# Stage A weights in runs of four columns, and loads moved ahead of the z writes, in a fused FFT-mixing and squared-ReLU kernel

## Chip, cores, metric

The kernel runs on one core of one Trainium2 chip. The metric is device time in microseconds (us), lower is better.

## The reference

x is (8, 3008, 256). It is filtered along the sequence in the frequency domain, then goes through a feed-forward layer:

```python
X = np.fft.rfft(x, axis=1)
Y = X * (filt_r + 1j * filt_i)[None, :, :]
y = np.fft.irfft(Y, n=3008, axis=1).astype(np.float32)      # (8, 3008, 256)
h = np.maximum(y.reshape(24064, 256) @ w_in, 0.0)           # 2048 wide
out = h * h @ w_out                                         # (24064, 256)
```

## The kernel before

The FFT of length 3008 = 64 x 47 is done by matmuls. Stage A transforms over 47, stage B over 64; the product with the filter follows, then stage P (back over 64) and stage y (back over 47). Between A and B and between P and y the data change their layout; for batches 1 to 7 both times through DRAM (u written to dU and read as ut; z written to dZ and read as zt), for batch 0 the first time on chip (uT, turned by TensorE). Batch 0 and part of batch 1 form a prologue. After it, slots of one eighth of a 512-token group follow each other: four matmuls of the first layer (`ffn_g1`), eight of the second for the group before (`ffn_g2`), a ReLU on ScalarE, a square on VectorE. The FFT of batch b+1 is woven into the slots of batch b by `fft_plan`: `put(r, place, unit, ...)` puts a unit into slot r.

Stage A of batch 0, whose casts out of PSUM the change touches:

```python
def chunk_a0(c):
    for k in range(2):
        for dt in range(2):
            if dt == 0:
                banks, _ = bank_pair(f"psA_0_{c}_{k}")       # psH: one tile of two banks; psF, psO: two tiles
            ps = banks[dt]
            for i in range(4):                               # 8 matmuls of 96 columns
                ...
                nc.tensor.matmul(o, xw16[(0, 2 * (c % 2))][:, m, d], s0[:, c // 2, :], start=True, stop=False)
                nc.tensor.matmul(o, xw16[(0, 1)][0:120, m, d], s0[0:120, 2 + c, :], start=False, stop=True)
            m = 32 * c + 16 * k
            o = uT[:, dt, :, m:m + 16].rearrange("p c (m q) -> p m q c", q=4)
            pv = ps[:, 0:384].rearrange("p (m q c) -> p m q c", m=4, q=4)
            if dt == 0: nc.scalar.copy(out=o, in_=pv)
            else:       nc.vector.tensor_copy(out=o, in_=pv)
```

The end of the prologue, and a frequency unit of batch 1 (twelve of them):

```python
for r in range(14):                          # filter, product and stage P of batch 0
    ...                                      # unit_p(0, p) writes z after every third p (4 writes)
    for k in {5: (0,), 8: (1, 2)}.get(r, ()):
        load_wide(1, k); cast_wide(1, k, nc.gpsimd)          # x of batch 1
    if r == 10:
        read_z(0, 0, (0,)); load_wout(0)
... # chunk_a(1, 0..3) between z reads, u writes, load_wout(1) and the first four unit_y(0, n)

def unit_b(b, p):
    ps = psF(...)                                            # two buffers, shared with stages P, y, A
    ... # two matmuls
    nc.vector.tensor_mul(out=prod, in0=ps..., in1=sF[...])
    if b > 0:
        swap = nc.gpsimd if b == 1 else nc.vector
        swap.tensor_copy(out=yf[0:64], in_=prod[64:128, 1])
        swap.tensor_copy(out=yf[64:128], in_=prod[0:64, 1])
def unit_s(b, p):                                            # in the same slot
    nc.vector.tensor_add(out=yf, in0=prod[:, 0], in1=yf)
```

Of the kernel before, what the change touches and what calls it, by code (L numbers as in the profile page):

```python
# [9 lines left out]
F16 = mybir.dt.float16  # L10
# [8 lines left out]
N1, N2, NC, NM = 64, 47, 24, 32  # L19
# [7 lines left out]
def _build_consts():  # L27
    N = N1 * N2
    n2 = np.arange(N2)
    m = np.arange(NM)  # L30


    SA = np.zeros((N2, 2, 2, 2, NC))
    for c in range(NC):
        for h in range(2):
            SA[:, h, h, 0, c] = np.cos(2 * np.pi * n2 * c / N2)
            SA[:, h, h, 1, c] = np.sin(2 * np.pi * n2 * c / N2)



    S0 = np.zeros((128, 6, 2, 48))
    for h in range(2):
        q = SA[:, h, h].reshape(N2, 48)
        for t in range(2):
            S0[2 * h + t::4, t, h] = q[:32]
        for c in range(4):
            S0[4 * h + c:120:8, 2 + c, h] = q[32:]


    freq = np.full((NC, 64), -1)  # L50
    for c in range(NC):
        for j in range(32):
            freq[c, j] = 47 * j + c
            if c:
                freq[c, 32 + j] = 47 * j + 47 - c
    freq[0, 32] = N // 2


    SB = np.zeros((NM, 2, 2, NC, 2, 64))

    n1j = 8 * (m % 8) + 2 * (m // 8)
    SP = np.zeros((2, 64, NC, 2, 2, NM))
    for c in range(NC):
        for f in range(64):
            k = freq[c, f]
            if k < 0:
                continue
            sg = 1.0 if (f < 32 or c == 0) else -1.0
            for h in range(2):
                th = 2 * np.pi * ((k * (32 * h + m)) % N) / N  # L70
                SB[:, h, 0, c, 0, f] = np.cos(th)
                SB[:, h, 1, c, 0, f] = -sg * np.sin(th)
                SB[:, h, 0, c, 1, f] = -np.sin(th)
                SB[:, h, 1, c, 1, f] = -sg * np.cos(th)
            if c == 0 and f == 32:
                SB[:, :, 1, c, :, f] = 0.0
            w = (1.0 if k in (0, N // 2) else 2.0) / N
            for i in range(2):
                th = 2 * np.pi * ((k * (n1j + i)) % N) / N
                cs, sn = w * np.cos(th), w * np.sin(th)  # L80
                SP[0, f, c, i, 0] = cs
                SP[0, f, c, i, 1] = sg * sn
                SP[1, f, c, i, 0] = -sn
                SP[1, f, c, i, 1] = sg * cs


    SY = np.zeros((32, 2, 2, N2, 2))
    for c in range(NC):
        th = 2 * np.pi * c * n2 / N2
        for i in range(2):  # L90
            SY[c + c // 12 * 4, i, 0, :, i] = np.cos(th)
            SY[c + c // 12 * 4, i, 1, :, i] = -np.sin(th)


    PF = np.zeros((128, 6, 2, 2, 32))
    for w, (s, q) in enumerate(PQ):
        for j in range(32):
            PF[4 * j + q, w, :, s, j] = 1.0

    SPx = SP.reshape(2, 64, -1)[::-1]  # L100
    f16 = lambda a, p: np.ascontiguousarray(a.reshape(p, -1).astype(np.float16))
    C0 = np.zeros((128, 896))
    C0[:, 0:576] = S0.reshape(128, 576)
    C0[0:94, 576:672] = SA.reshape(94, 96)
    C0[:, 672:766] = SY.reshape(128, 94)
    C0[:, 768:896] = np.eye(128)
    return f16(C0, 128), f16(PF, 128), f16(SB, 128), f16(SP, 128), f16(SPx, 128)


@with_exitstack  # L110
def kernel(
# [9 lines left out]
    nc = tc.nc  # L121
# [77 lines left out]



    sC0 = const.tile([128, 896], F16, name="sC0")
    nc.scalar.dma_start(out=sC0, in_=dC0.ap())
    s0 = sC0[:, 0:576].rearrange("p (w q) -> p w q", q=96)
    sSA = sC0[0:94, 576:672]
    sSY = sC0[0:112, 672:766]
    ident = sC0[:, 768:896]
# [44 lines left out]
    nc.vector.memset(sign[64:128], -1.0)  # L252


    zero = const.tile([128, 512], F16, name="zero")
    nc.vector.memset(zero, 0.0)

    def keep_warm(n):
        ps = psO("warm").rearrange("p a d -> p (a d)")
        for _ in range(n):  # L260
            nc.tensor.matmul(ps, zero[:, 0:128], zero, start=True, stop=True)

    nc.scalar.copy(out=zero[0:1, 0:1], in_=zero[0:1, 1:2])
    keep_warm(14)


    sF = const.tile([128, 2, NC, D], F16, name="sF")
# [48 lines left out]
        nc.sync.dma_start(out=w32s[2][:, c, :],  # L316
                          in_=moe_w_out.rearrange("(jt r) c -> r jt c", r=128)[:, c, :])

    def cast_wout(k, eng=nc.vector):
        c = slice(4 * k, 4 * k + 4)  # L320
        eng.tensor_copy(out=sWout[:, c, :], in_=w32s[2][:, c, :])


    x16s, us, uts, prods, zes, zts, yts = {}, {}, {}, {}, {}, {}, {}
# [11 lines left out]
    def unit_a(b, a):  # L336

        c, i = divmod(a, 4)
        if i == 0:
            us[(b, c)] = p_u.tile([96, 8, D], F16, tag="u", name=f"u_{b}_{c}")  # L340
        ps = psF(f"psA_{b}_{a}")
        nc.tensor.matmul(ps[0:96, :], sSA, x16s[(b, c)][:, 2 * i:2 * i + 2, :],  # L342
                         start=True, stop=True)
        o = us[(b, c)][:, 2 * i:2 * i + 2, :]
        pv = ps[0:96, :].rearrange("p (a d) -> p a d", d=D)
        if a % 2 == 0:
            nc.scalar.copy(out=o, in_=pv)  # L347
        else:
            nc.vector.tensor_copy(out=o, in_=pv)  # L349
        if i == 3:  # L350
            write_u(b, c)

    def chunk_a(b, c):

        u = p_u.tile([96, 8, D], F16, tag="u", name=f"u_{b}_{c}")
        us[(b, c)] = u
        for k in range(2):
            banks, groups = bank_pair(f"psA_{b}_{c}_{k}")
            for i in range(2):
                m = slice(4 * k + 2 * i, 4 * k + 2 * i + 2)  # L360
                o = banks[i][0:96]
                nc.tensor.matmul(o, s0[:, c // 2, :], xw16[(b, 2 * (c % 2))][:, m, :],
                                 start=True, stop=False)
                nc.tensor.matmul(o, s0[0:120, 2 + c, :], xw16[(b, 1)][0:120, m, :],
                                 start=False, stop=True)
            eng = pair_engine()
            for t, i in groups:
                n = t.shape[1]
                o = u[:, 4 * k + 2 * i:4 * k + 2 * i + 2 * n, :]
                pv = t[0:96].rearrange("p t (a d) -> p (t a) d", d=D)  # L370
                if eng is nc.scalar:
                    eng.copy(out=o, in_=pv)
                else:
                    eng.tensor_copy(out=o, in_=pv)
# [5 lines that stand above are left out]
# [9 lines left out]
                    nc.tensor.matmul(o, xw16[(0, 1)][0:120, m, d], s0[0:120, 2 + c, :],  # L389
                                     start=False, stop=True)  # L390
                m = 32 * c + 16 * k
                o = uT[:, dt, :, m:m + 16].rearrange("p c (m q) -> p m q c", q=4)
                pv = ps[:, 0:384].rearrange("p (m q c) -> p m q c", m=4, q=4)
                if dt == 0:
                    nc.scalar.copy(out=o, in_=pv)  # L395
                else:
# [89 lines left out]
    def unit_y(b, n):  # L486
# [11 lines left out]
                yps[0] = psH(f"psY_{b}_{n}")  # L498
            ps = yps[0][:, dt, :]
        if prologue[0]:  # L500
            nc.tensor.matmul(ps[:, 0:D], zero[:, 0:128], zero[:, 0:D], start=True, stop=True)
        for jj in range(4):
            nc.tensor.matmul(ps[:, 94 * jj:94 * jj + 94],  # L503
                             zt[:, 4 * (g % 2) + jj, dt * 128:(dt + 1) * 128],
# [70 lines left out]
    def fft_plan(b):  # L575
# [6 lines left out]
        if b == 1:  # L582
            for n in range(4, 16):
                put(n - 1 if n < 8 else 10 + n // 2 if n < 12 else 4 * n - 31, n % 2,
                    unit_y, 0, n)
            for k in range(2, 4):
                put(2 + k, 1, cast_wout, k)
        t0 = 6
        for a in range(0 if b > 1 else 16, 16):
            put(t0 + a // 2, a % 2, unit_a, b, a)  # L590
        put(4 if b == 1 else 14, 1, read_u, b)
        t0 = 8 if b == 1 else 18
        for p in range(12):
            r = t0 + (25 if b == 1 else 19) * p // 11
            put(r, 0, unit_b, b, p)
            put(r, 0, unit_s, b, p)
            put(r + 2, 1, unit_p, b, p)
# [48 lines left out]
    uts[0] = p_ut.tile([128, NC, D], F16, tag="ut", name="ut_0")  # L646
    for k in range(6):
        turn_u(k)
    for k, eng in enumerate((nc.vector, nc.scalar, nc.vector)):
        place_f(0, k, eng)  # L650
    place_f(1, 0, nc.scalar)
    for r in range(14):
        if r < 12:
            unit_b(0, r)
        if r < 10 and r % 2 == 0:
            place_f(1, r // 2 + 1, nc.scalar)
        if r < 6 and r % 2 == 1:
            place_f(0, r // 2 + 3, nc.scalar)
        if r >= 2:
            unit_p(0, r - 2)  # L660
        for k in {5: (0,), 8: (1, 2)}.get(r, ()):
            load_wide(1, k)
            cast_wide(1, k, nc.gpsimd)
        if r == 10:
            read_z(0, 0, (0,))
            load_wout(0)
    for k in range(2):
        cast_wout(k, nc.gpsimd)
    read_z(0, 1, (0,))
    chunk_a(1, 0)  # L670
    chunk_a(1, 2)
    for c in range(2):
        read_z(0, c, (1,))
    write_u(1, 0)
    chunk_a(1, 1)
    write_u(1, 2)
    load_wout(1)
    for n in range(2):
        unit_y(0, n)
    chunk_a(1, 3)  # L680
    for n in range(2, 4):
        unit_y(0, n)
    prologue[0] = False
    write_u(1, 1)
    write_u(1, 3)
    for c in range(2, 4):
        read_z(0, c)

# [48 lines left out]
```

## Time and profile before

| | kernel before |
|---|---|
| median of 3 runs, us | 832.46 (829.75 to 833.49) |
| span of the profiled run | 829.0 |
| first ReLU of the feed-forward part | 82.80 |
| slot 8 begins / slot 34 begins / slot 56 begins | 91.87 / 147.97 / 194.70 |

A slot is taken to begin with its ReLU on ScalarE. The page's first lines follow (span; then for each engine busy us, share of the span, instructions). PE is TensorE and PEld its weight loads, DVE is VectorE, ACT ScalarE, POOL GpSimd:

```profile
span 829.0 us, 14766 instructions
PE 790.5 (95%) x6086; PEld 559.4 (67%) x6086; DVE 553.9 (67%) x869; ACT 564.8 (68%) x708; POOL 37.1 (4%) x51
```

TensorE is busy for 95 % of the span.

### The profile page before, as it was taken

How to read it: one execution, taken by the hardware profiler on the slowest of the kernel's cores; microseconds unless marked ns; L12 is line 12 of the kernel's file. 1: busy time of each engine (PE TensorE's matmuls, PEld its weight loads, DVE VectorE, ACT ScalarE, POOL GpSimd, SP SyncE). 2: the span in 40 equal slices, each digit the busy share in tenths (PEclk: the TensorE clock that was granted, in tenths of full speed). 3: DMA queues.
4: the chain of work that ended last, by engine and by line, in shares of the span. 5: the costliest groups of instructions: out<-in, count | busy, mean ns of one | idle time of the engine just before them, and what ended most of it. 6: DMA issues, size and time to landing. Idle time of an engine off the chain costs nothing.

```text
span 829.0 us, 14766 instructions
## 1 busy us (share of the span) xinstructions
PE 790.5 (95%) x6086; PEld 559.4 (67%) x6086; DVE 553.9 (67%) x869; ACT 564.8 (68%) x708; POOL 37.1 (4%) x51
## 2 busy tenths in 40 slices
PE   5686989999999999999999999999999999999998
PEld 3563566666767667786767766786767766676666
DVE  5672766656995589756995579755996569654332
ACT  4572766676777777776777767777777767766663
POOL 4202122000000000000000000000000000000000
PEclk7597999999999999999999999999999999999999
DMA  9449416724563356625555336815556242331111
GB/s 365 172 147 272 153 51 173 173 64 153 141 183 84 102 153 160 172 57 160 153 140 115 95 122 166 201 42 152 145 146 153 64 153 77 101 79 39 39 40 51
DMA packets 87947, 107.95 MB, mean 130 GB/s; under 512 B 6224, under 2 KB 78672, under 8 KB 83408
## 3 DMA queue, kind: packets, MB, share of 16 engines
q1 hardware_dynamic: 87528, 106.59, 45.2%
q8 instruction: 47, 0.77, 0.4%
q10 hardware_dynamic: 288, 0.43, 0.2%
q14 instruction: 20, 0.16, 0.1%
q0 software_dynamic: 64, 0.00, 0.0%
HBM read 58.76 MB, written 48.23 MB: 129 GB/s over the span
## 4 chain that ended last, share of the span: by engine, by line
PE 83%; DMA 6%; DVE 6%; ACT 2%; POOL 1%; issue 1%; SPq 0%; DVEq 0%; POOLq 0%; ACTq 0%
PE psO L548 36%; PE psH L533 35%; PE psA L342 3%; PE psY L503 2%; PE psB L426 2%; DMA ut<-dU 2%; PE psP L462 2%; DVE prod L429 2%; DVE h L541 2%; DMA dZ<-ze 2%; ACT uT L395 1%; DMA xw<-in_x_dram 1%; DMA zt<-dZ 1%; POOL yf L438 1%; POOL yf L437 1%; DVE uT L397 1%
## 5 line engine op out<-in xcount | busy, mean ns | idle before, releaser
L537 ACT ACTIVATE h<-psH 128x1024 f16<-128x1024 f32 x376 | 385.1, 1025 | 191.3 <-PE psH L533 191.3
L548 PE MATMUL psO<-sWout,h 128*128 128x256 f16 x3008 | 388.9, 272 | 0.1
L533 PE MATMUL psH<-yt,sWin 128*128 128x512 f16 (+7 forms) x1728 | 387.1, 351 | 1.9 <-DVE yt L512 1.0
L548 PEld LDWEIGHTS <-h 128*128 128x128 f16 x3008 | 290.6, 98 | 77.9 <-DVE h L541 0.4
L541 DVE TENSOR_TENSOR h<-h 128x1024 f16<-128x1024 f16 x376 | 253.5, 685 | 99.8 <-ACT h L537 98.5
L533 PEld LDWEIGHTS <-sWin 128*128 128x128 f16 x1728 | 159.6, 98 | 101.7 <-issue 3.7
L429 DVE TENSOR_TENSOR prod<-psB,sF 128x1024 f16<-128x1024 f32 x96 | 116.7, 1220 | 10.7 <-PE psB L426 7.6
L512 DVE CAST yt<-psY 128x376 f16<-128x376 f32 x64 | 35.1, 549 | 59.9 <-PE psY L503 55.2
L464 ACT CAST ze<-psP 128x512 f16<-128x512 f32 x96 | 56.0, 586 | 23.3 <-PE psP L462 20.0
L349 DVE CAST u<-psA 96x512 f16<-96x512 f32 x48 | 33.0, 687 | 45.1 <-PE psA L342 45.1
L555 ACT COPY ost<-psO 128x512 f32<-128x512 f32 x94 | 55.4, 589 | 7.7 <-PE psO L548 6.2
L444 DVE TENSOR_TENSOR yf<-prod,yf 128x512 f16<-128x512 f16 x84 | 35.7, 425 | 19.4 <-POOL yf L438 17.0
L503 PE MATMUL psY<-sC,zt 112*128 112x94 f16 x512 | 42.6, 206 | 5.5 <-DMA zt<-dZ 5.3
L503 PEld LDWEIGHTS <-zt 112*128 112x128 f16 x512 | 35.2, 98 | 18.2 <-DMA zt<-dZ 4.8
L426 PE MATMUL psB<-ut,sSB 128*128 128x256 f16 x192 | 36.6, 272 | 2.7 <-DMA ut<-dU 1.3
L342 PE MATMUL psA<-x,sC 94*96 94x512 f16 x96 | 36.6, 382 | 0.0
L426 PEld LDWEIGHTS <-sSB 128*128 128x128 f16 x192 | 18.6, 98 | 23.9 <-issue 4.9
L462 PE MATMUL psP<-yf,sSP 128*128 128x256 f16 x168 | 32.1, 273 | 2.7 <-DVE prod L429 1.8
L510 ACT CAST yt<-psY 128x376 f16<-128x376 f32 x64 | 29.8, 467 | 6.0 <-issue 5.1
L328 DVE CAST x<-x 94x2048 f16<-94x2048 f32 x24 | 29.2, 1217 | 0.0
L347 ACT CAST u<-psA 96x512 f16<-96x512 f32 x48 | 27.5, 572 | 0.0
L395 ACT CAST uT<-psA 128x384 f16<-128x384 f32 x8 | 14.5, 1996 | 13.8 <-PE psA L389 13.8
(56 smaller groups left out, 289.9 us busy)
## 6 DMA issues: line engine op xcount, KB each, us to landing
x<-in_x_dram SPq DMA_DIRECT2D x20, 768.0 KB
dZ<-ze SPq DMA_DIRECT2D x32, 384.0 KB
zt<-dZ SPq DMA_DIRECT2D x64, 192.0 KB
dU<-u SPq DMA_DIRECT2D x28, 384.0 KB
out_dram<-ost SPq DMA_DIRECT2D x32, 256.0 KB
out_dram<-ost SPq DMA_DIRECT2D x64, 128.0 KB
ut<-dU SPq DMA_DIRECT2D x7, 1024.0 KB
xw<-in_x_dram SPq DMA_DIRECT2D x6, 1024.0 KB
```

Source lines behind the costliest of these rows:

```text
L342: nc.tensor.matmul(ps[0:96, :], sSA, x16s[(b, c)][:, 2 * i:2 * i + 2, :], start=True, stop=True)
L426: nc.tensor.matmul(ps[:, i * D:(i + 1) * D], sSB[:, 2 * p + i, :], uts[b][:, 2 * p + i, :], start=True, stop=True)
L429: nc.vector.tensor_mul(out=prod, in0=ps.rearrange("p (a d) -> p a d", d=D).unsqueeze(1).to_broadcast([128, 2, 2, D]), in1=sF[:, :, 2 * p:2 ...
L444: nc.vector.tensor_add(out=yf, in0=prod[:, 0], in1=yf)
L462: nc.tensor.matmul(ps[:, i * D:(i + 1) * D], sSP[:, c2, :], prod[:, i, :], start=True, stop=True)
L464: nc.scalar.copy(out=zes[(b, c)][:, 2 * i6:2 * i6 + 2, :], in_=ps.rearrange("p (a d) -> p a d", d=D))
L503: nc.tensor.matmul(ps[:, 94 * jj:94 * jj + 94], zt[:, 4 * (g % 2) + jj, dt * 128:(dt + 1) * 128], sSY, start=True, stop=True)
L533: nc.tensor.matmul(ps[:, i, o:o + n], sWin[:, dt, jt * 128:(jt + 1) * 128], yts[b][:, dt, r:r + n], start=(dt == 0), stop=(dt == 1))
L537: nc.scalar.activation(out=h2[:, 2 * s:2 * s + 2, :], in_=ps, func=AF.Relu)
L541: nc.vector.tensor_mul(out=v, in0=v, in1=v)
L548: nc.tensor.matmul(pso[g][:, t % 2, :], h2s[g][:, jt, t * 128:(t + 1) * 128], sWout[:, jt, :], start=(jt == 0), stop=(jt == NJT - 1))
L555: nc.scalar.copy(out=ost, in_=pso[g])
```

## The change

The change has three intents: let the casts of batch 0's stage A write runs of four elements, and keep the clock up to it; fetch and cast all of batch 1's x and of W_out before the z writes, so that no load stands between those; and move the fourth chunk of batch 1's stage A out of the prologue into the slots, which makes its u, and so the twelve frequency units, later.

```diff
-    C0[:, 0:576] = S0.reshape(128, 576)
+    C0[:, 0:576] = S0.reshape(128, 6, 2, 2, NC).transpose(0, 1, 4, 2, 3).reshape(128, 576)
+    C0[:, 896:1472] = S0.reshape(128, 576)          # s1, the old order, for batch 1
...
-    keep_warm(14)            # matmuls of 512 columns
+    keep_warm(125)           # of 128 columns
...
-                o = uT[:, dt, :, m:m + 16].rearrange("p c (m q) -> p m q c", q=4)
-                pv = ps[:, 0:384].rearrange("p (m q c) -> p m q c", m=4, q=4)
+                o = uT[:, dt, :, m:m + 16].rearrange("p c (m q) -> p m c q", q=4)
+                pv = ps[:, 0:384].rearrange("p (m c q) -> p m c q", m=4, q=4)
...                                                   # fft_plan, b == 1
-            for k in range(2, 4):
-                put(2 + k, 1, cast_wout, k)           # was on VectorE
+        t0 = 2 if b == 1 else 6
+        for a in range(12 if b == 1 else 0, 16):      # fourth chunk: slots 8 and 9
             put(t0 + a // 2, a % 2, unit_a, b, a)
-        put(4 if b == 1 else 14, 1, read_u, b)
-        t0 = 8 if b == 1 else 18
+        put(10 if b == 1 else 14, 1, read_u, b)
+        t0 = 14 if b == 1 else 18
         for p in range(12):
-            r = t0 + (25 if b == 1 else 19) * p // 11
+            r = t0 + 19 * p // 11
...                                                   # prologue, ahead of the filter
+    for k in range(3):
+        if k == 2:
+            load_wout(0)
+        load_wide(1, k)
+        cast_wide(1, k, nc.gpsimd)
+    load_wout(1)
+    for k in range(4):
+        cast_wout(k)                                  # all on GpSimd
...                                                   # the loads inside and after the loop are gone;
+    for c in (0, 2, 1):                               # three chunks, then z reads, u writes, four y units
+        chunk_a(1, c)
```

More of the change, by code (lines that the diff above doesn't have):

```diff
@@ L101, in _build_consts @@
     f16 = lambda a, p: np.ascontiguousarray(a.reshape(p, -1).astype(np.float16))
-    C0 = np.zeros((128, 896))
-    C0[:, 0:576] = S0.reshape(128, 576)
+    C0 = np.zeros((128, 1472))
+    C0[:, 0:576] = S0.reshape(128, 6, 2, 2, NC).transpose(0, 1, 4, 2, 3).reshape(128, 576)
+    C0[:, 896:1472] = S0.reshape(128, 576)
     C0[0:94, 576:672] = SA.reshape(94, 96)
@@ L198, in load_x @@
         x32s[(b, c)] = t
-    sC0 = const.tile([128, 896], F16, name="sC0")
+    sC0 = const.tile([128, 1472], F16, name="sC0")
     nc.scalar.dma_start(out=sC0, in_=dC0.ap())
     s0 = sC0[:, 0:576].rearrange("p (w q) -> p w q", q=96)
+    s1 = sC0[:, 896:1472].rearrange("p (w q) -> p w q", q=96)
     sSA = sC0[0:94, 576:672]
@@ L252 @@
     nc.vector.memset(sign[64:128], -1.0)
-    zero = const.tile([128, 512], F16, name="zero")
+    zero = const.tile([128, 128], F16, name="zero")
     nc.vector.memset(zero, 0.0)
@@ L260, in keep_warm @@
         for _ in range(n):
-            nc.tensor.matmul(ps, zero[:, 0:128], zero, start=True, stop=True)
+            nc.tensor.matmul(ps[:, 0:128], zero, zero, start=True, stop=True)
     nc.scalar.copy(out=zero[0:1, 0:1], in_=zero[0:1, 1:2])
-    keep_warm(14)
+    keep_warm(125)
     sF = const.tile([128, 2, NC, D], F16, name="sF")
@@ L317, in load_wout, with cast_wout @@
                           in_=moe_w_out.rearrange("(jt r) c -> r jt c", r=128)[:, c, :])
-    def cast_wout(k, eng=nc.vector):
+    def cast_wout(k):
         c = slice(4 * k, 4 * k + 4)
-        eng.tensor_copy(out=sWout[:, c, :], in_=w32s[2][:, c, :])
+        nc.gpsimd.tensor_copy(out=sWout[:, c, :], in_=w32s[2][:, c, :])
     x16s, us, uts, prods, zes, zts, yts = {}, {}, {}, {}, {}, {}, {}
@@ L341, in unit_a @@
         ps = psF(f"psA_{b}_{a}")
-        nc.tensor.matmul(ps[0:96, :], sSA, x16s[(b, c)][:, 2 * i:2 * i + 2, :],
-                         start=True, stop=True)
+        m = slice(2 * i, 2 * i + 2)
+        if b == 1:
+            nc.tensor.matmul(ps[0:96, :], s1[:, c // 2, :], xw16[(b, 2 * (c % 2))][:, m, :],
+                             start=True, stop=False)
+            nc.tensor.matmul(ps[0:96, :], s1[0:120, 2 + c, :], xw16[(b, 1)][0:120, m, :],
+                             start=False, stop=True)
+        else:
+            nc.tensor.matmul(ps[0:96, :], sSA, x16s[(b, c)][:, m, :], start=True, stop=True)
         o = us[(b, c)][:, 2 * i:2 * i + 2, :]
@@ L361, in chunk_a @@
                 o = banks[i][0:96]
-                nc.tensor.matmul(o, s0[:, c // 2, :], xw16[(b, 2 * (c % 2))][:, m, :],
+                nc.tensor.matmul(o, s1[:, c // 2, :], xw16[(b, 2 * (c % 2))][:, m, :],
                                  start=True, stop=False)
-                nc.tensor.matmul(o, s0[0:120, 2 + c, :], xw16[(b, 1)][0:120, m, :],
+                nc.tensor.matmul(o, s1[0:120, 2 + c, :], xw16[(b, 1)][0:120, m, :],
                                  start=False, stop=True)
@@ L500, in unit_y @@
         if prologue[0]:
-            nc.tensor.matmul(ps[:, 0:D], zero[:, 0:128], zero[:, 0:D], start=True, stop=True)
+            for k in range(2):
+                nc.tensor.matmul(ps[:, 128 * k:128 * k + 128], zero, zero, start=True, stop=True)
         for jj in range(4):
@@ L585, in fft_plan @@
                     unit_y, 0, n)
-            for k in range(2, 4):
-                put(2 + k, 1, cast_wout, k)
-        t0 = 6
-        for a in range(0 if b > 1 else 16, 16):
+        t0 = 2 if b == 1 else 6
+        for a in range(12 if b == 1 else 0, 16):
             put(t0 + a // 2, a % 2, unit_a, b, a)
-        put(4 if b == 1 else 14, 1, read_u, b)
-        t0 = 8 if b == 1 else 18
+        put(10 if b == 1 else 14, 1, read_u, b)
+        t0 = 14 if b == 1 else 18
         for p in range(12):
-            r = t0 + (25 if b == 1 else 19) * p // 11
+            r = t0 + 19 * p // 11
             put(r, 0, unit_b, b, p)
@@ L660 @@
             unit_p(0, r - 2)
-        for k in {5: (0,), 8: (1, 2)}.get(r, ()):
-            load_wide(1, k)
-            cast_wide(1, k, nc.gpsimd)
         if r == 10:
             read_z(0, 0, (0,))
-            load_wout(0)
-    for k in range(2):
-        cast_wout(k, nc.gpsimd)
     read_z(0, 1, (0,))
-    chunk_a(1, 0)
-    chunk_a(1, 2)
+    for c in (0, 2, 1):
+        chunk_a(1, c)
     for c in range(2):
         read_z(0, c, (1,))
-    write_u(1, 0)
-    chunk_a(1, 1)
-    write_u(1, 2)
-    load_wout(1)
-    for n in range(2):
-        unit_y(0, n)
-    chunk_a(1, 3)
-    for n in range(2, 4):
+    for c in (0, 2, 1):
+        write_u(1, c)
+    for n in range(4):
         unit_y(0, n)
     prologue[0] = False
-    write_u(1, 1)
-    write_u(1, 3)
     for c in range(2, 4):
```

## The prediction

> **What bounds the kernel now.** The row of 40 slices on the page comes first: TensorE is busy nine tenths or more from the fifth slice (20.7 us each) to the end, and only the first four show lower digits.
>
> ```profile
> PE   5686989999999999999999999999999999999998
> PEclk7597999999999999999999999999999999999999
> ```
>
> So the time is a prologue of some 82 us plus 747 us of feed-forward work in which TensorE hardly rests; a change of the prologue counts in full, if it costs nothing behind it. The chain of waits over the first 90 us shows what the prologue is made of.
>
> ```profile
> 10.80 1.87 ACT uT L395
> 12.71 0.24 PE psA L387
> ...
> 17.58 5.30 ACT uT L395 x3
> ...
> 27.22 5.29 DVE uT L397 x3
> 32.55 4.35 PE psT L405 x39
> ...
> 39.25 1.24 DVE sF L297
> ...
> 60.77 0.59 ACT ze L464
> ...
> 62.79 9.69 DMA dZ<-ze
> 72.54 3.30 DMA zt<-dZ
> 75.88 0.50 PE psY L503 x4
> ```
>
> Two parts are no TensorE work. From 10.3 to 32.5 us stage A of batch 0 waits for casts of 128x384 out of PSUM, about 1.87 us each, while casts of nearly the same size elsewhere take a quarter of it (groups of the page):
>
> ```profile
> L512 DVE CAST yt<-psY 128x376 f16<-128x376 f32 x64 | 35.1, 549 | 59.9 <-PE psY L503 55.2
> ...
> L395 ACT CAST uT<-psA 128x384 f16<-128x384 f32 x8 | 14.5, 1996 | 13.8 <-PE psA L389 13.8
> ```
>
> From 61.4 to 75.9 us everything waits for the last z write and the read after it. The write took 9.69 us; a write of the same size at 151.41 us took 2.78. Before it in the queue stood x of batch 1 and half of W_out.
>
> Behind the prologue I read batch 1's frequency stage, because the change re-times it:
>
> ```profile
> 95.05 1.29 DVE h L541 x2
> 96.34 1.15 DVE prod L429
> 97.48 0.05 issue
> 97.53 0.61 POOL yf L437
> 98.19 0.62 POOL yf L438
> 98.83 0.42 DVE yf L444
> 99.26 1.20 DVE h L541 x2
> ```
>
> VectorE multiplies (prod), then stands still for 1.35 us (97.48 to 98.83) while GpSimd swaps halves, then adds: 2.92 us a unit, and 0.60 per square.
>
> [...] The slow cast walks c innermost, [...]; the yt cast writes runs of four. [...] 1.87 us for 384 lone elements, 0.47 (ScalarE, the group of L510) and 0.55 us for 376 in runs. [...] the warm matmuls' weight loads start 0.427 us apart (3.56, 3.99, 4.41), the granted clock reads 0.5 from 11 to 38.3 us, and stage A's matmuls follow at 0.046 us around 10.3 and at 0.080 later. [...]
>
> **The change, part by part.**
>
> *Constants and warm-up.* The constant row grows from 1792 to 2944 bytes, 147 KB more; at the 420 GB/s of the first slices 0.35 us, so x is cast at about 10.6 instead of 10.3 us. The warm-up goes from 14 matmuls of 512 columns to 125 of 128: 0.107 us each at half clock (a quarter of 0.427)[...]. With the clock rising at 7.6 us as in this trace, 41 run cold and 84 warm[...]; the moment of the rise can differ, so 11.8 to 13.4, and I take 12.6. Stage A thus starts 2.3 us later than before, but warm.
>
> *Stage A.* 128 matmuls at 0.046 = 5.9 us. In four of the eight bank pairs the second half waits for the cast of the first, as before; each such wait is now cast 0.5 + drain and hand-over 0.27 = 0.77, in all 3.1. The last VectorE cast adds 0.7. Transposes start at 12.6 + 9.7 = 22.3 us instead of 32.55. Six warm transposes' evictions (1.0 to 1.3 us each on two engines) then let the first filter cast begin 5.1 us later instead of 6.7: 27.4 instead of 39.25, a gain of 11.85 us.
>
> *Filter and products of batch 0.* Unchanged, 39.25 to 61.36 = 22.1 us, so the last z copy would end at 49.5. The loads that now go first reach into this: x and W_out, 5 MB at 2.6 to 3.1 us each, can start only as the W_in buffers come free (GpSimd casts end near 31.4 and 33.9 us), and the third x load only after the first one's cast, near 39.7. Their data then end near 47. The first z write stands behind them and lands near 49, and the fourth z tile reuses its buffer (three buffers): its copy, due at 46.9, waits about 2 us, of which I charge 1. Last z copy: 50.5.
>
> *The z round trip.* Last write issued at about 51.4 (the read before it in the queue waits for the second write), landing 3.2 later, read 3.4: first y matmul at about 58.1 instead of 75.88. The three remaining chunks of stage A (24 matmuls x 0.216 = 5.2 us) fill the wait. Then four y units at full clock: the first activation 3.4 us later, at 61.5, where it was 82.80 (6.9 later, with chunk 3 at half clock between). **Prologue: 21.3 us saved.**
>
> *Given back behind it.* Chunk 3 moves into slots 8 and 9: 8 x 0.216 = 1.7 us of TensorE. And batch 1's twelve units start in slot 14 instead of 8 but still end in slot 33. Before, from the first product (92.05) to the last sum (150.2) were 58.1 us, beginning 9.25 us after the first activation: 67.4 in all. Now slot 14 begins after 9.1 + 6 x 1.74 + 1.7 = 21.3 us, its product after 22.6, or 23.2 if the u round trip (dU write 4.07, read 3.87, ordered from slot 9 on) holds it. From there VectorE alone needs 12 x 2.92 + 19 squares x 0.60 + 4 y casts x 0.46 + 2 x casts x 1.14 = 50.6 us; TensorE needs only about 40 (19 x 1.74 + 12 x 0.44 + 8 x 0.17). With 1 us of friction: 23.0 + 51.4 = 74.4. **Given back: 7 us.** The last sum releases batch 1's z write, read and y units in both kernels, so the loss can't be caught up in slots 34 to 38. Moving two W_out casts from VectorE to GpSimd (1.2 us) lies beside ScalarE-bound slots and is worth nothing.
>
> Sum: 832.5 - 21.3 + 7 = 818.2; I say 817.5, leaning a little to the side where z isn't held up.
>
> **The rivals.**
> 1. *Batch 1 does not become VectorE's.* TensorE would then pay only 1.7 us, and recover some of its 5 us of idle time there: 811 to 813. For it: later batches use the same 19-slot spacing and lose nothing. Against it: there VectorE swaps for itself; batch 1 alone has the GpSimd standstill, and it already filled VectorE's time to 54 of 58 us.
> 2. *The clock falls back.* Stage A at 0.080 us and cold transposes: about +6 us, 824. Against it: cutting the timeline into the 3.4 us steps in which the clock changes, it fell after steps with TensorE busy 0.43 or less and held at 0.74 or more; stage A should be near 0.7. Nothing in the trace lies between.
> 3. *z stays queued behind the loads.* If loads slip by 4 us, the z buffers stall ScalarE longer: 821. If they go faster, 815.
> 4. *Runs of four don't help fully, the step of 256 bytes being the cause.* At 0.9 us a cast: +2 us. No cast in the trace has this step with runs of four.
>
> **Range and chances.** Prologue 21.3 +- 3 (start of warm clock 0.8, casts 1, z queue 2), given back 7 +- 1.5, and a tail for a cold clock: 8 in 10 between 810 and 825. Faster by over 2% means under 815.8 us, about half a deviation below my value: 0.35. Slower needs a fault I don't see: 0.01.
>
> **What would show it.** Casts of uT at 0.5 to 0.6 us; transposes starting near 22; no load between the z writes and a last z write of about 3 us; first activation near 61.5. Then slots 14 to 33 lasting some 50 us against 40 of TensorE work, with VectorE's standstill before each sum on the chain. Slots of 2.0 us there would prove my loss wrong, and a granted clock of 0.5 after 12 us my stage A.

At the marks, what the author had from elsewhere than a trace of this case is cut: reasons for the slow casts, for the write held up behind loads, for the standstill and for the clock's rise, and the time of a 128-column matmul at full clock with the sum that used it. The warm-up sum read 3.16 + 4.4 + 4.7 = 12.3 us, from which 12.6 was taken, its last term 84 matmuls at full clock. The 12.6, and the 22.3, 27.4 and 21.3 saved that build on it, are the author's estimate. Half of the 0.107 us measured at half clock would give 84 x 0.0535 = 4.5 and so 12.1; the changed kernel's trace has these matmuls 0.056 us apart at full clock. Two more figures are estimates: 0.27 us of drain and hand-over (in the trace 0.24 us from the start of the last matmul to the cast, 10.56 to 10.80, and 0.05 from the end of the cast to the next matmul), and 2.6 to 3.1 us a load (W_in's two halves of 1 MB landed 2.5 us apart, 29.00 and 31.47).

## More of the kernel before

For batch 1's frequency stage, from its first product to its last sum, the busy time of each engine stands in this line (stretch, its length, then busy us and instructions of PE, PEld, DVE, ACT, POOL; granted clock; DMA):

```profile
92.05:150.20 58.15, 54.82 (x407) 37.74 (x406) 38.30 (x57) 38.48 (x49) 14.69 (x24) 1.00 0.36 98
```

VectorE looks two thirds busy. It isn't free for the rest: twelve times it waits 1.4 us for GpSimd's swap, 17 us of the 20 that it isn't busy. The prediction's chain shows one such wait.

## The result, and the profile after

| | before | changed |
|---|---|---|
| median, us | 832.34 (4 runs) | 820.28 (818.77 to 821.68, 4 runs) |
| ratio | | 0.9859, 95 % interval 0.9829 to 0.9889 |
| span of the profiled run | 829.0 | 819.2 |

A ratio is the mean time of one kernel's runs over that of the other's of the same rounds, so it isn't quite the ratio of the medians. The gain is 1.4 %, inside 2 %. (The two profiled runs differ by 9.8 us, the medians by 12: single runs scatter by 2 us and more, and the profiled run of the kernel before was one of its faster ones, 830.75.) The page of the changed kernel:

```profile
span 819.2 us, 14996 instructions
PE   7979898999999999999999999999999999999998
PEclk9989998999999999999999999999999999999999
```

A slice is 20.5 us now. TensorE's row is fuller in the first, second and fourth slices, but the fifth and the seventh, both in batch 1's frequency stage, have an 8 where the kernel before had a 9 (its slices are 20.7 us, so they don't cover quite the same work); the clock row has lost its 5 and has an 8 in the third slice and in that seventh. The chain of waits over the prologue (start, length, what):

```profile
3.15 9.98 PE warm L263 x125
...
13.53 0.49 ACT uT L403
...
21.83 0.57 DVE uT L405
...
22.45 0.58 PE psT L413 x7
...
27.17 1.24 DVE sF L299
...
39.48 9.02 DMA dZ<-ze
48.60 0.59 ACT ze L472
...
51.66 3.45 DMA dZ<-ze
55.13 3.43 DMA zt<-dZ
...
58.61 0.34 PE psY L512 x4
```

Set beside the prediction's chain: the casts fell from 1.87 to 0.48 and 0.57 us, the transposes begin at 22.45 instead of 32.55, the filter at 27.17 instead of 39.25. (These are places on the chain; the very first transposes start at 22.00 and 31.41.) The last z write takes 3.45 us instead of 9.69. A new wait stands in the middle: the first z write, behind the moved loads, lands at 48.50, and ScalarE waits 2.44 us for its buffer. ScalarE's timeline gives the first ReLU:

```profile
62.83 1.02 ACT L546 ACTIVATE h<-psH 128x1024 f16<-128x1024 f32 x1 [2.80 <-PE psH L542]
```

62.83 where it was 82.80: the prologue is 20.0 us shorter. But slot 56 begins at 185.15 where it began at 194.70: only 9.5 us are left there, and 9.8 at the end. **10.4 us went between the first ReLU and slot 56.** The stretch from the first product to the last sum of batch 1 is now this one:

```profile
84.62:140.90 56.28, 47.10 (x330) 31.33 (x329) 34.88 (x50) 31.83 (x42) 14.63 (x24) 0.94 0.41 110
```

It is 2 us shorter than before, but begins 21.8 us after the first ReLU instead of 9.2. TensorE has 9.2 us of idle time in it where it had 3.3, and a granted clock of 0.94. VectorE's 56.2 us are 34.8 busy, 16.9 of waiting for swaps, 2.5 of waiting for TensorE's psB and 1.9 for ScalarE's ReLU. Two slots stand out in ScalarE's starts: slot 15 with 6.2 us and slot 29 with 7.2, where two are usual. The chain across slot 29:

```profile
122.45 0.42 DVE yf L452
122.88 0.60 DVE h L550
123.48 1.13 DVE x L330
124.61 0.60 DVE h L550
125.21 1.15 DVE prod L437
...
126.41 0.61 PE psP L470 x2
127.02 1.71 PE psH L542 x4
```

TensorE's psP needs the PSUM buffer that the product (prod) reads last; the product stands behind a square, an x cast and another square, and these behind the wait for a swap. TensorE waits 3.6 us for it, and then its four psH matmuls take 1.71 us instead of 0.86: the granted clock is 0.5 from 125.2 to 132.0 us.

### The profile page after: what moved, and what is told of

The parts are those of the page before. It is cut to its first block, busy times and chain, and to the rows that moved or that the text cites. A ratio compares the mean times of both kernels' runs of the same rounds, so it can differ in the third digit from the quotient of the medians.

```text
span 819.2 us, 14996 instructions
## 1 busy us (share of the span) xinstructions
PE 790.1 (96%) x6201; PEld 560.9 (68%) x6201; DVE 543.3 (66%) x868; ACT 553.9 (68%) x709; POOL 38.9 (5%) x53
## 4 chain that ended last, share of the span: by engine, by line
PE 86%; DMA 5%; DVE 4%; ACT 2%; POOL 1%; issue 0%; ACTq 0%; POOLq 0%; DVEq 0%
PE psO L557 37%; PE psH L542 36%; PE psA L351 3%; PE psY L512 2%; PE psB L434 2%; DMA dZ<-ze 2%; PE psP L470 2%; DMA ut<-dU 2%; DVE prod L437 1%; DMA zt<-dZ 1%; PE warm L263 1%; DVE h L550 1%; ACT h L546 1%; POOL yf L446 1%; POOL yf L445 1%; DVE yf L452 0%
## 5 line engine op out<-in xcount | busy, mean ns | idle before, releaser
L472 ACT CAST ze<-psP 128x512 f16<-128x512 f32 x96 | 55.8, 585 | 26.9 <-PE psP L470 22.3
L521 DVE CAST yt<-psY 128x376 f16<-128x376 f32 x64 | 35.0, 548 | 58.2 <-PE psY L512 56.5
L452 DVE TENSOR_TENSOR yf<-prod,yf 128x512 f16<-128x512 f16 x84 | 35.7, 425 | 19.4 <-POOL yf L446 16.9
L445 DVE COPY yf<-prod 64x512 f16<-64x512 f16 x72 | 20.8, 289 | 2.5
```

Of the source, the lines that this page charges most:

```text
L472: nc.scalar.copy(out=zes[(b, c)][:, 2 * i6:2 * i6 + 2, :], in_=ps.rearrange("p (a d) -> p a d", d=D))
```

## The experiments

Twelve runs, all correct. Times are medians of four runs; the ratio is to the kernel before of the same rounds. "First ReLU", "stretch" (first product to last sum of batch 1) and slot lengths are from the profiled run.

| run | time, us | ratio (95 %) | first ReLU | last sum after it | stretch |
|---|---|---|---|---|---|
| before | 832 | 1 | 82.8 | 67.4 | 58.2 |
| changed | 820.28 | 0.9859 (0.9829 to 0.9889) | 62.8 | 78.0 | 56.2 |
| a_vecswap | 813.05 | 0.9769 (0.9753 to 0.9785) | 63.9 | 68.3 | 47.0 |
| a_latesum | 814.96 | 0.9793 (0.9777 to 0.9809) | 64.1 | 70.9 | 49.3 |
| a_early4 | 811.50 | 0.9743 (0.9726 to 0.9761) | 64.6 | 67.3 | 58.1 |
| a_yspread | 816.15 | 0.9808 (0.9787 to 0.9828) | 62.6 | 72.1 | 50.3 |
| b_latesum | 829.63 | 0.9971 (0.9956 to 0.9986) | 84.4 | 65.2 | 56.0 |
| a_no_runs | 830.28 | 0.9953 (0.9905 to 1.0001) | 73.7 | 77.5 | 55.3 |
| a_warm56 | 818.34 | 0.9834 (0.9795 to 0.9873) | 62.0 | 76.4 | 55.1 |
| a_loads_between | 825.74 | 0.9911 (0.9879 to 0.9944) | 66.7 | 78.1 | 56.1 |
| a_wout_late | 818.76 | 0.9826 (0.9796 to 0.9856) | 60.5 | 77.9 | 55.3 |
| c_early_vec | **808.53** | 0.9710 (0.9693 to 0.9727) | 65.1 | 62.5 | 53.3 |
| c_all_vec | 809.29 | 0.9724 (0.9688 to 0.9760) | 64.0 | 65.8 | 53.6 |
| c_all_late | 809.69 | 0.9739 (0.9709 to 0.9769) | 61.5 | 67.6 | 55.6 |

My theory was that the prologue's gain is real and that VectorE's standing still for GpSimd, packed into fewer slots, gives part of it back. The rival was that the loss has another cause: the order of y units and buffers, or the clock.

### Where the time was given back

**a_vecswap**: VectorE swaps for itself, as it does for all later batches.

```diff
-            swap = nc.gpsimd if b == 1 else nc.vector
+            swap = nc.vector
```

> The changed kernel, with the half swaps of batch 1 done by VectorE instead of GpSimd. Theory (what is given back behind the prologue is VectorE standing still for each GpSimd swap, more often per slot now): a unit costs VectorE 1.15 + 2 x 0.29 + 0.42 = 2.15 us instead of 2.92 with the standstill, its need from the first product to the last sum falls from 50.6 to 41.3 us, about TensorE's 40; that stretch, 56 us in the changed kernel, should be 42 to 46 us, and the time 807 to 811 us. Rival (the late start or the order of y units and PSUM buffers, not the standstill): the stretch stays above 52 us and the time above 816.

The stretch fell from 56.2 to 47.0 us, the last sum came 9.7 us earlier relative to the first ReLU. The rival's 52 us are out. Part of the gain, some 2 us by an estimate under a_yspread, is the clock, which stays at 1.00. VectorE does more work (two copies of 0.29 us a unit) in less time, as this line of the same stretch shows; compare 34.88 busy of 56.28 above:

```profile
85.20:132.20 47.00, 42.71 (x322) 29.79 (x320) 42.18 (x74) 31.43 (x41) 0.00 (x0) 1.00 0.46 128
```

My numbers were a little too good (42 to 46 us, 807 to 811): slots 15 and 29 are still 4.7 and 4.1 us long, so the order of y units and PSUM buffers has a share, as the rival said.

**a_latesum**: no work is moved, only the order; each sum is issued one slot after its product.

```diff
-            put(r, 0, unit_s, b, p)
+            put(r + 1 if b == 1 else r, 0, unit_s, b, p)
```

> The changed kernel, with each sum of batch 1 issued one slot after its product, so that VectorE squares while GpSimd swaps; no work is taken away. Theory (standstill): VectorE's need is 12 x 1.57 + 15.5 = 34.3 us, below TensorE's 40; first product to last sum 41 to 45 us plus up to one slot, time 806 to 811. Rival (it is VectorE's amount of work, not its standing still): no gain, 819 to 821.

The stretch fell to 49.3 us: that standing still costs time is shown, since here the amount of work is the same. But it missed the 41 to 45 us, and the timeline of VectorE says why:

```profile
98.23 1.23 DVE L437 TENSOR_TENSOR prod<-psB,sF 128x1024 f16<-128x1024 f32 x1 [0.21 <-PE psB L434]
99.37 0.68 DVE L550 TENSOR_TENSOR h<-h 128x1024 f16<-128x1024 f16 x1
101.21 0.43 DVE L452 TENSOR_TENSOR yf<-prod,yf 128x512 f16<-128x512 f16 x1 [1.16 <-POOL yf L446]
```

The square (h) now runs inside the wait, yet 1.16 us of waiting remain, where 1.4 less 0.6 should. GpSimd's first swap takes longer beside the square: its mean from 85 to 140 us is 914 ns here and 611 ns in the changed kernel. Why it does isn't shown by this run, only that it does and by how much. I had not reckoned with that.

**a_early4**: the fourth chunk goes back into the prologue, into the wait for z, and the units start in slot 8 and are spread over 25 slots again.

```diff
-    for c in (0, 2, 1):
-        chunk_a(1, c)
+    chunk_a(1, 0); write_u(1, 0)
+    for c in (2, 1, 3):
+        chunk_a(1, c)
...
-        put(10 if b == 1 else 14, 1, read_u, b)        # and t0 = 14, 19 slots
+        put(4 if b == 1 else 14, 1, read_u, b)         # and t0 = 8, 25 slots
```

> The changed kernel with stage A's fourth chunk back in the prologue, inside the wait for z, and batch 1's twelve units from slot 8 on again, 25 slots long, as before the change. Theory (the shorter span for the twelve units costs what is given back): first activation stays within 0.5 us of 62.8, first activation to last sum is 67 to 68 us as before the change instead of 78, time 809 to 812. Rival (the loss comes from elsewhere, such as W_out's casts or the clock falling by chance): time above 816.

The last sum comes 67.3 us after the first ReLU, as before the change (67.4): the whole of what was given back is back. Its cause is what this edit undoes: the units' late start and their packing into 19 slots, with the fourth chunk's 1.7 us in the slots; the run doesn't separate these. Only the first ReLU was worse than expected, 64.6 where I had allowed up to 63.3: the fourth chunk's cast waited for the first chunk's u write to free its buffer (dU, 3.76 us on the chain up to 62.57). Time 811.5, as predicted.

**a_yspread**: y units 8 to 15 go into slots without a frequency unit.

```diff
-                put(n - 1 if n < 8 else 10 + n // 2 if n < 12 else 4 * n - 31, n % 2,
+                put(n - 1 if n < 8 else n + 2 if n < 12 else (16, 18, 21, 25)[n - 12], n % 2,
```

> The changed kernel with y units 8 to 15 of batch 0 moved into slots without a frequency unit (10 to 13, 16, 18, 21, 25), no work changed. Theory (the part of the given-back time that the sum of VectorE work did not hold, 4 to 5 us, comes from y casts queued behind a GpSimd swap in slots 15 and 29, each of which stops TensorE): slots 15 and 29 fall from 6 and 7 us to 3 to 4, first product to last sum 51 to 53 us instead of 56, time 815 to 818. Rival (TensorE stops there whatever stands in the queue): 820.

The stretch fell to 50.3 us, slots 15 and 29 to 2.0 and 2.6, though slots 31 and 33 grew to 3.7 and 4.4:

```profile
84.37:134.70 50.33, 44.10 (x317) 29.26 (x316) 33.43 (x49) 31.19 (x40) 14.63 (x24) 1.00 0.44 119
```

That is a sharper result than I expected (51 to 53 us). VectorE's 33.4 us of work and its 16.9 us of waiting for swaps now fill the stretch, and its waits for TensorE and ScalarE, 4.4 us in the changed kernel, are gone. The stretch isn't quite the same work: four y units, and so two of the four y casts (1.1 us), now lie before it. So the y units in the units' slots are what brought those waits, by their place in VectorE's queue and in the two PSUM buffers; the run doesn't tell these two apart. The clock didn't fall in this run's stretch. What its fall at 125 us cost the changed kernel can be estimated from runs with the same order of slots: a_no_runs, a_warm56 and a_wout_late have one step of 3.4 us at half clock in the stretch and take 55.1 to 55.3 us, the changed kernel and a_loads_between have two and take 56.2 and 56.1. That is about 0.9 us a step, so some 2 us of the changed kernel's stretch. This run lies 0.5 % of the kernel before below the changed one (0.9808 and 0.9859).

**b_latesum**: the edit of a_latesum, in the kernel before.

```diff
-            put(r, 0, unit_s, b, p)
+            put(r + 1 if b == 1 else r, 0, unit_s, b, p)
```

> The kernel before, with the same one-slot delay of the sums. Theory (the standstill already cost the kernel before some 4 to 6 us between slots 8 and 34): first product to last sum 51 to 54 us instead of 58.1, time 826 to 829. Rival (before the change the standstill was hidden): 832.

The stretch lost 2.2 us and the time 0.3 %, short of what I expected (51 to 54 us and 826 to 829), though the gain is clear of noise: the kernel before was bound by TensorE nearly as much as by VectorE (54.82 us busy of 58.15 above), so the standstill cost it little (2.2 us of the stretch here). It is dear where the units are packed (6.9 us in a_latesum).

### The parts of the prologue

**a_no_runs**: the old column order of the weights and the old cast, the rest as changed.

```diff
-    C0[:, 0:576] = S0.reshape(128, 6, 2, 2, NC).transpose(0, 1, 4, 2, 3).reshape(128, 576)
+    C0[:, 0:576] = S0.reshape(128, 576)
-                o = uT[...].rearrange("p c (m q) -> p m c q", q=4)
+                o = uT[...].rearrange("p c (m q) -> p m q c", q=4)         # and pv likewise
```

> The changed kernel with the old column order of batch 0's stage A weights, so that the casts write lone 2-byte elements again; all else as changed. Theory (runs of four took some 10 us out of the path): casts at 1.87 us, transposes begin at 34 to 36 us instead of 22.45, the wait for a z buffer goes away, first activation at 72 to 75 us, time 829 to 832. Rival (with a warm clock and a fuller TensorE the casts no longer bound stage A): transposes before 28 us, time below 825.

As the theory said: the chain has casts of 1.88 us again, the transposes at 33.3 us (34 to 36 expected), and the first ReLU came 10.9 us later than in the changed kernel.

```profile
13.00 1.88 ACT uT L403
...
33.27 4.35 PE psT L413 x39
```

The time is 830.3: without the runs of four, hardly anything of the gain is left, as the rest of the prologue's gain is about what the slots give back.

**a_loads_between**: the loads of x and W_out back in their old places.

```diff
-    for k in range(3): ... load_wide(1, k) ...         # and load_wout(0), load_wout(1) ahead of the filter
+        for k in {5: (0,), 8: (1, 2)}.get(r, ()):
+            load_wide(1, k); cast_wide(1, k, nc.gpsimd)
+        if r == 10: load_wout(0)                       # load_wout(1) behind the u writes
```

> The changed kernel with x of batch 1 and W_out loaded between the z writes as before the change (all of W_out cast by GpSimd). Theory (the last z write behind 3 MB of loads cost 6 to 8 us): last z write 8 to 10 us, first y matmul 6 to 8 us later than 58.6, first activation at 69 to 71 us, time 826 to 829. Rival (the wait for a z buffer and chunks that now come after it eat the gain of the new order): time 820 to 822.

The last z write took 9.51 us again:

```profile
48.56 9.51 DMA dZ<-ze
58.14 3.51 DMA zt<-dZ
61.70 0.50 PE psY L512 x4
```

But the first ReLU is only 3.9 us later (66.7), less than my 6 to 8: in this run the clock rose 3 us sooner, so the filter began at 25.7 us instead of 27.2, and the wait for a z buffer is gone (last z copy done at 47.9 us against 50.5). Expected 826 to 829, measured 825.7. The order of the loads is worth some 4 us (ratios 0.9911 and 0.9859, whose intervals just overlap), and by an estimate from the filter's start 1.4 us more, if the earlier rise of the clock isn't the edit's doing.

**a_warm56**: as many warm-up columns as before, in matmuls of 128.

```diff
-    keep_warm(125)
+    keep_warm(56)
```

> The changed kernel with 56 warm-up matmuls of 128 columns instead of 125, which is the number of columns of before. Theory (the long warm-up is needed to carry the full clock into stage A): stage A starts near 10.6 us instead of 13.2, but falls to half clock within it; transposes begin at 23 to 25 us, time 821 to 824. Rival (stage A is now dense enough to keep the clock by itself, and the extra warm-up only delays it): granted clock stays 1.0, transposes begin near 20 us, time 817 to 819.

Each theory was right for one step of the clock. Stage A began at 10.6 us; the table by stretches (PE busy is the second number, the granted clock the one after POOL's) shows the clock fall after a step with 1.50 us of 3.40 busy, and rise again after the next:

```profile
8.70:12.10 3.40, 1.50 (x28) 1.24 (x27) 1.30 (x2) 0.48 (x1) 0.00 (x0) 1.00 1.04 440
12.10:15.50 3.40, 2.83 (x38) 2.69 (x35) 1.44 (x3) 0.96 (x2) 2.42 (x3) 0.50 0.99 418
15.50:18.90 3.40, 2.27 (x47) 2.05 (x45) 1.35 (x3) 1.44 (x3) 3.08 (x3) 1.00 0.99 407
```

The transposes began at 21.05 us, 1.4 sooner than with the long warm-up. Three of four runs are at 818.1 to 818.5, in the rival's range, one at 823.0; the intervals overlap. The long warm-up isn't shown to help, and isn't shown to hurt.

**a_wout_late**: W_out is loaded behind the u writes; only x stays ahead of the z writes.

```diff
-        if k == 2: load_wout(0)                         # and load_wout(1) after the loop
...
     for c in (0, 2, 1): write_u(1, c)
+    for k in range(2): load_wout(k)
+    for k in range(4): cast_wout(k)
```

> The changed kernel with only x of batch 1 ahead of the z writes; W_out is loaded after the writes of u, behind the first z reads. Theory (2 MB of W_out ahead of the first z write are what makes ScalarE wait from 46.2 to 48.6 us for a z buffer): no such wait, last z copy near 48, first activation at 59.5 to 61.5, time 817 to 819. Rival (the wait costs nothing because the second z write holds the queue anyway, or W_out comes too late): 820 or more.

ScalarE's wait for a z buffer is gone, the last z copy ends at 49.1 instead of 50.5, and the first ReLU comes at 60.5, 2.3 us sooner. The median is only 1.5 us lower, and the intervals overlap, so a gain isn't shown. The profile shows where it goes: slot 7 lasts 3.7 us instead of 1.5. W_out's casts on GpSimd now run beside the squares, and on the chain one square took 1.45 us instead of 0.69. So W_out ahead of the z writes does cost a wait of 2 us (2.44 in the changed kernel), and putting it later costs nearly as much elsewhere.

Taken back one at a time, the parts cost at the first ReLU 10.9 us (runs of four, a_no_runs), 3.9 us (loads, a_loads_between) and 1.7 us (the fourth chunk, a_early4): 16.5 of the 20.0 us. They aren't independent (each shifts the clock and the z buffers for the others), and the rest is not assigned.

### Versions

**c_early_vec** is a_early4 with a_vecswap's edit. **c_all_vec** adds a_yspread's idea (y units 8 to 15 in slots 9, 11, 11, 13, 15, 18, 22, 25) and loads the second half of W_out behind the u writes. **c_all_late** is c_all_vec with a_latesum's edit in place of a_vecswap's. The edits beyond those shown, for the last two:

```diff
-                put(n - 1 if n < 8 else 10 + n // 2 if n < 12 else 4 * n - 31, n % 2,
+                put(n - 1 if n < 8 else (9, 11, 11, 13, 15, 18, 22, 25)[n - 8], n % 2,
...
-    load_wout(1)                                       # ahead of the filter
     for c in (2, 1, 3): write_u(1, c)
+    load_wout(1)                                       # and its two casts
```

> Fourth chunk in the prologue, units from slot 8, and swaps by VectorE. Theory: the two gains add as far as TensorE allows; VectorE needs 12 x 2.15 + 15.6 + 4.1 = 45.5 us where TensorE needs 50; first product to last sum 53 to 55 us instead of 58, time 806 to 809. Rival (early units leave nothing to gain): 811.

> As c_early_vec, with y units 8 to 15 kept out of the slots of units and the second half of W_out loaded behind the writes of u. Theory: no wait for a z buffer (1 to 2 us), stretch 52 to 53 us: 804 to 807. Rival (the late W_out cast on GpSimd holds up the squares, as it did in the run with all of W_out late): 808 or more.

> As c_all_vec, but swaps stay on GpSimd and each sum comes one slot after its product. Theory: VectorE is freed of the swaps and needs 12 x 1.57 + 19.7 = 38.5 us; stretch 52 to 54 us, time within 1.5 us of c_all_vec. Rival [...]: 3 us or more slower than c_all_vec.

c_early_vec came as expected: stretch 53.3 us, TensorE idle 0.75 us in it, 808.5 us; 2.9 % below the kernel before, where the change alone is 1.4 % below, with an interval far from its own. The medians of the other two missed. Their stretches are free of idle TensorE time too, but slot 8 lasts 5.7 and 5.2 us, because the read of u stands behind the late half of W_out in the queue (that read is on the chain for 9.2 us in c_all_vec; the u writes are ahead of W_out). The four runs of c_all_vec fall into two pairs, 806.5 and 806.7, which is in the expected range and below every run of c_early_vec, and 811.9 and 812.0; the profiled run is of the slower pair, and no trace shows what the faster one did. So the rival's guess, 808 or more, holds for the median alone, and the squares that it named aren't what the chain shows. c_all_late is within 1.5 us of it, as expected.

## Why the prediction was right, point by point

The number (817.5; measured 820.28) held, and so did the mechanism: a gain in the prologue, and a loss where VectorE stands still. But the gain was put 1.3 us too high and the loss 3.4 us too low; the errors add up and don't cancel, and the lean from 818.2 to 817.5 went the wrong way. The 20.0 and 10.4 us below are read from two profiled runs, 9.8 us apart; the medians are 12.1 apart, so one of the two is some 2 us off for typical runs. a_early4 speaks for the loss: undoing it brings 8.8 us in the medians, although its first ReLU is 1.7 us later.

- *Warm-up and stage A.* Start 12.6 us predicted, the last warm-up matmul ended at 13.1 (the clock rose at 9.1 us and not at 7.6); casts 0.5, measured 0.48 (ScalarE) and 0.57; transposes 22.3, measured 22.45; first filter cast 27.4, measured 27.17. The clock kept full speed through stage A (granted 1.00 from 13.1 to 22.0 us, TensorE busy for 6.43 of 8.90), so rival 2 did not come about there; it fell later, at 50.1 us after the wait for a z buffer, and at 60.3 (TensorE busy for 0.43 and 0.34 of the 3.4 us before). Rival 4, the 256-byte step, is out: the step is the same, and the cast took 0.48 us where the rival had 0.9.
- *Loads and z.* The wait for a z buffer came as reckoned: first z write landing near 49, measured 48.50; last z copy 50.5, measured 50.45; last z write 51.4, measured 51.66; first y matmul 58.1, measured 58.61. Rival 3 is out.
- *First ReLU.* 61.5 predicted, 62.83 measured. 0.5 us of the difference was there at the first y matmul, 0.8 lies in the last step: four y units and the first layer were taken at full clock, 3.4 us, and took 4.2, as the clock had fallen to half at 60.3 us, after the step in which TensorE waited for z. **Prologue 21.3 predicted, 20.0 measured.**
- *Given back.* 7 us predicted, 10.4 measured (10.5 up to the last sum). The first product came 21.8 us after the first ReLU (predicted 22.6, or 23.2 if the u round trip held it, so it did not); the stretch from there was 56.2 us and not 51.4. The mis-sized term is the "1 us of friction" on top of VectorE's sum of 50.6. VectorE's own work and standstills were 51.7 us, close to the sum (each standstill measured 1.41 us, not 1.35), so rival 1 is out; its waits for TensorE and ScalarE were 4.4 us. a_yspread shows what these were made of: y units in the units' slots. The half clock of 125 to 132 us is part of it, some 2 us by the estimate there. The sum of VectorE's work was a floor here, and the waits that items bunched into one slot brought came on top of it.
- *Slips in its reading.* The row of TensorE before the change has an 8 in the sixth slice, so it isn't nine tenths from the fifth slice on throughout. "Held at 0.74 or more" leaves out a step of the same trace at 0.69 (120.2 to 123.6 us) in which the clock held. For its 23.0 + 51.4 its own terms give 22.6 or 23.2, and 51.6. None of these moves the result by more than half a microsecond. And the slots of the two W_out casts on VectorE are not ScalarE's alone: from 86.9 to 92.0 us VectorE was busy for 5.09 of 5.10 us and ScalarE for 4.57.
- *W_out casts moved off VectorE, worth nothing.* Not tested by itself.

That the loss comes from late, packed units that stand still is shown twice: by undoing the lateness (a_early4) and by taking away the standstill (a_vecswap), each of which brings the time down by 7 us or more. Not settled is how much of the loss is the fallen clock; 2 us is an estimate.

## What to carry to other kernels

When a change pulls a part of a stage out of a prologue, look at what waits for that stage, and count for the later stretch what the engine needs in order, standstills included; a share of busy time of two thirds can be a full engine (VectorE here: 38.30 busy and 17.0 of standing still in 58.15 us). Here a cast into a layout with a 256-byte step fell from 1.87 us to 0.48 and 0.56 us once its innermost run had four 2-byte elements, and reordering the weights' columns of the matmul before made that run; the price was a second copy of these weights, 147 KB, for batch 1. The loads put ahead of a write in the same queue didn't vanish here: the write behind them landed at 48.5 us and held ScalarE for 2.44 us, and where half of W_out was put behind the u writes, the next read was on the chain for 9.2 us (u in c_all_vec).

## What these traces show of casts, clock and contention

- *Casts.* Here 384 lone 2-byte elements at a 256-byte step took 1.86 to 2.2 us on ScalarE and VectorE alike, 4.9 ns each at the least; the same elements at the same step in runs of four took 0.48 us on ScalarE and 0.56 on VectorE, 1.25 and 1.45 ns each. These two patterns were measured, and no run length between or beyond them.
- *Clock.* The records of the two kernels, before and changed, start at 7.59 and 9.12 us; up to there a window of the profile reads 1.00, though the warm matmuls of 512 columns were 0.427 us apart, and 0.217 at the end, and those of 128 columns 0.107, and then 0.056. From there to 140 us the recorded clock changed only at the ends of 3.41 us steps. It fell to 0.5 after the six steps at full clock with TensorE busy for 0.43 of the time or less, and after none of those with 0.48 or more; it rose after the six steps at half clock with 0.90 or more, and after none with 0.75 or less (busy as the profile models it). a_warm56 above has a fall after 0.44 and a rise after 0.83.
- *Gaps.* In the kernel before, TensorE's longest gap in the step from 7.6 to 11.0 us was 1.7 us (8.57 to 10.28), and the clock fell at 11.0, with TensorE busy for 0.43 of the step.
- *Contention.* In a_latesum the first GpSimd swap beside squares took 914 ns in the mean of twelve, where it takes 611 in the changed kernel; in a_wout_late a square beside GpSimd's W_out cast took 1.45 us instead of 0.69. What the two engines wait for in each other isn't shown.
